# Two blocks per job transposed on VectorE in 32x32 parts and laid in place by transfers within SBUF

## The chip, the cores and the metric

One core of a Trainium2 chip runs the whole program as one launch. The metric is the time of one execution on the device in microseconds (us); the number before is the median of three runs. The engines are named as in the profile: PE is TensorE, PEld its loading of the stationary operand (it overlaps PE), DVE is VectorE, ACT is ScalarE, POOL is GpSimd, SP is SyncE, which here only issues transfers.

## The reference

Attention with a threshold, then two MLP layers, all in float32. Attention has 4 batches of 8 heads, 576 positions and 64 values per head; the MLPs have 2304 tokens, a model width of 512 and an inner width of 2048.

```
scores = q @ k.T / sqrt(64)
thresh = scores.max(-1) - tau
scores = where(scores >= thresh, scores, -1e9)
attn = exp(scores - scores.max(-1))
attn = attn / (attn.sum(-1) + 1e-9)
x = attn @ v                      # heads side by side: 2304 x 512
h = x @ w_in;  g = h if h >= 1, 0 if h <= -1, else (h + 1)**2 / 4;  x = g @ w_out
h = x @ w_in2; g = h * clip(h + 3, 0, 6) / 6;                        out = g @ w_out2
```

## The kernel before, in words

**Jobs, blocks, steps.** Attention is cut into 16 jobs, numbered from 0: a batch and a pair of heads each. A job has five blocks of query rows: four of 128 rows with both heads, and a last one with the 64 remaining rows of both heads. A step of the loop in `attention()` starts one block: step 5j+i starts block i of job j. Within a step, `em_scores` multiplies q by k on TensorE into two double banks P0 and P1 of PSUM (from job 10 on, JR, in three products of split operands), and VectorE moves the result to the tile p, with the row's extreme as a by-product (L395). `em_exp` lets ScalarE take the exponential (L408) and VectorE form the threshold (L411). `em_mask` multiplies by the threshold's mask on VectorE and sums the rows (L417). The tile p has three buffers and holds two heads of 2 x 288 columns; it has one query row on each partition.

**Turning a block.** The product with v needs the block transposed. A step later `em_pt` does this, once per head: four transposes of 128x128 on TensorE against the identity (issued by the helper `turn`, L294) into one bank of PSUM, and an evacuation by ScalarE (L445) into the tile Gf of the job's group. Group "a" holds blocks 0 and 1 (256 queries), group "b" blocks 2 to 4 (320). The last 64 key columns of both heads are turned by `em_tail` (L459, L463) into Gt. The banks Q0 and Q1 are taken by turns (`rotate`) by `em_pt`, `em_tail` and the product with v.

**The product with v.** When the last block of a group is turned, its five chunks go into the queue `pvq`: four chunks of 128 keys and the tail, each with one product per head (L481). `pv_chunk` runs them, and ScalarE moves the result to xu (L487). Gf and Gt have one buffer per group, so `turned` first runs what is left of the job before. `pv_run(5)` stands twice in a step, and a chunk runs at the earliest in the step behind the one that queued it. The normalisation (`pre_norm`, `fetch_norm`, `em_norm`) follows in steps 5j+5, 5j+6 and 5j+9; the row sums go through DRAM (L507, L522, L524).

**What runs beside attention.** Once the first batch is through, the first MLP layer (`dense1`) runs in between: at each `yield` of `attention()` it gets 0.57 credits (`share`), and pays 0.33 for each piece that it emits. A round works on 256 tokens; one value f of the inner width (an f-step) has twelve products into the one bank Q2 (`em_h`, L724), then ScalarE, VectorE (L735), ScalarE and POOL (L742) on the result, and twelve products of the output layer (`em_part`, L786) into Q3. There are 60 f-steps; what is left of them when attention ends runs behind it, followed by the rest of the first MLP and the second.

**What sets the order.** The Tile framework orders the instructions of each engine, in general by their place in the program, earlier where what stands before them is not ready. `pe_pins` lists attention's products in order; products of the MLP may not come before the last but one of them at the time of their emission, those with v not before the last. Scores after the first of a block are raised in priority. Each engine works through its queue in order.

**Queues.** All transfers here are issued by SP, in order. Loads of q and k for the job after the next are cut into strips of 32 columns (L233), since from job 4 on VectorE turns q and k in 32x32 parts (L304 for jobs from 10 on, 128x640). Loads of v are L281 and L282, stores of the first layer's partial sums L800.

**The tile w_c** in the pool `stage` has two buffers of 128x512 and serves the split of the MLP's weights (`split_a`, `split_b`). The weights that the first rounds need are split before job 10; the next ones follow behind attention.

Of the kernel before, what the change touches and what calls it, by code (L numbers as in the profile page):

```python
# [8 lines left out]
F32 = mybir.dt.float32  # L9
# [9 lines left out]
def kernel(  # L19
# [12 lines left out]
    nc = tc.nc  # L32
    V, S, G, T = nc.vector, nc.scalar, nc.gpsimd, nc.tensor
    NB, NH, SEQ, D = q.shape
# [4 lines left out]
    MAIN = 512  # L39
    TAIL = SEQ - MAIN  # L40
# [7 lines left out]
    NF1 = 10  # L48
    NAT = 1
    JT = 4  # L50
    JR = 10
    MLAG = 2
    RAW = 3
# [4 lines left out]
    stage = ctx.enter_context(tc.tile_pool(name="stage", bufs=1))  # L58
# [138 lines left out]
    NBLK = 5  # L197
    HEADS = range(2)
# [4 lines left out]
    AFTER = {1: "a", 4: "b"}  # L203
# [13 lines left out]
    vn = [ap.tile([128, 5, 2, D], F32, name=f"vn{i}") for i in range(2)]  # L217
# [22 lines left out]
    def load_q(j):  # L240
# [4 lines left out]
        for h in HEADS:  # L245
            src = q[b, 2 * hp + h]
            if j >= JR:
                strips(qn, 0, src[0:MAIN, :], h)
                strips(qn, 16 + 2 * h, src[MAIN:SEQ, :], h)
                continue  # L250
            if j >= JT:
                strips(qn, 0, src, h)
# [100 lines left out]
    zt, gt, xu, p_t = {}, {}, {}, {}  # L353
# [59 lines left out]
    def em_mask(j, i):  # L413
        p, nm, th, es = blk.pop((j, i))
        for x, e in enumerate(es):
            z = zcol(x, i)
            pins["M"] = V.scalar_tensor_tensor(out=p[:, x], in0=p[:, x], scalar=th[:, x:x + 1], in1=e,  # L417
                                            op0=ALU.is_le, op1=ALU.mult, accum_out=zt[j][:, z:z + 1])
        p_t[j, i] = p.rearrange("p h e n -> p (h e n)")

    def turned(j, g):
        if (g, j) not in gt:
            n = GROUPS[g][0]
            while (g, j - 1) in gt:
                pv_chunk()
            gt[g, j] = (ap.tile([128, 2, 4, n], F32, tag=f"G{g}", name="Gf"),
                        ap.tile([128, n], F32, tag=f"T{g}", name="Gt"))
        return gt[g, j]

    def rotate():  # L430
        mode["r"] = 1 - mode.get("r", 0)
        return bank(f"Q{mode['r']}")

    def em_pt(j, i, h):

        p = p_t[j, i]
        g, d0 = PARTS[i]
        f = turned(j, g)[0]
        mode["n"] += 1
        tm = rotate() if mode["mlp"] else bank("Q0" if mode["n"] % 2 else "Q2")  # L440
        p0 = h * (SEQ + TAIL)
        for cc in range(4):
            turn(tm[:, cc * 128:(cc + 1) * 128], p[:, p0 + cc * 128:p0 + (cc + 1) * 128], cc == 0)
        if i < NBLK - 1:
            S.activation(out=f[:, h, :, d0:d0 + 128], in_=tm.rearrange("p (c n) -> p c n", c=4), func=ACTF.Copy)  # L445
        else:
            for x in HEADS:
                S.activation(out=f[:, x, :, d0:d0 + TAIL],
                                      in_=tm.rearrange("p (c h n) -> p h c n", c=4, h=2)[:, x], func=ACTF.Copy)
# [16 lines left out]
    o_t, pvq = {}, []  # L466

    def pv_chunk():

        j, g, c = pvq.pop(0)  # L470
        n, d0 = GROUPS[g]
        f, t = gt[g, j]
        if c == 0:
            if j not in xu:
                here.pop(j - XLIVE, None)
                xu[j] = here[j] = mt.tile([128, SEQ], F32, tag="xu", name="xu", bufs=XLIVE)
            o_t[j, g] = rotate() if mode["mlp"] else bank("Q1")
        o = o_t[j, g][:, 0:n]
        for h in (1, 0):
            with tc.high_priority(offset=0 if h else 900):  # L480
                mm = T.matmul(o[h * D:(h + 1) * D], vn[j % 2][:, c, h, :], f[:, h, c] if c < 4 else t,  # L481
                              start=(c == 0), stop=(c == 4), skip_group_check=True)
            after(mm, pe_pins[-1] if h else prev)
            prev = mm
        if c == 4:
            del gt[g, j], o_t[j, g]
            S.activation(out=xu[j][:, d0:d0 + n], in_=o, func=ACTF.Copy)  # L487
# [28 lines left out]
    def fetch_norm(j):  # L516
        if j not in rbs or j not in OVER:
            return
        rd, rb = rbs[j]
        for h in HEADS:  # L520
            r = slice(64 * h, 64 * h + 64)
            nc.sync.dma_start(out=rb[r, 0:MAIN].rearrange("p (c n) -> p c n", c=4),  # L522
                              in_=rd[4 * h:4 * h + 4, :].unsqueeze(0).to_broadcast([64, 4, 128]))
            nc.sync.dma_start(out=rb[r, MAIN:SEQ], in_=rd[8:9, r].to_broadcast([64, 64]))  # L524
# [35 lines left out]
    def attention():  # L560

        order = [(j, i) for j in range(NJ) for i in range(NBLK)]
        n = len(order)
        turns, tailq, maskq = [], [], []
        plan = {}

        def at(t, what, *x):
            plan.setdefault((t, what), []).append(x)

        for j in range(NJ):  # L570
            at(NBLK * j + (4 if j < HP - 1 else 3), "q", j + 1)
            at(NBLK * j + 4, "k", j + 1)
            at(NBLK * j + NBLK + 0, "z", j)
            at(NBLK * j + NBLK + 1, "f", j)
            at(NBLK * j + NBLK + 4, "n", j)

        def now_at(what):
            return plan.get((t, what), [])

        def masked():  # L580
            while maskq:
                b = maskq.pop(0)
                em_mask(*b)
                turns.append(b)
                tailq.append(b)

        def due(lag):
            r = []
            while turns and (len(turns) > lag or t >= n):
                r.append(turns.pop(0))  # L590
            return r

        def tails(lag):
            while tailq and (len(tailq) > lag or t >= n):
                em_tail(*tailq.pop(0))

        for t in range(n + 6):
            mode["t"] += 1
            mode["step"] = True
            if not mode["mlp"]:  # L600
                if t < n:
                    em_scores(*order[t])
                    maskq.append(order[t])
                pv_run(2)
                yield
                if t < n:
                    em_exp(*order[t], 0)
                    em_exp(*order[t], 1)
                masked()
                for x in now_at("z"):  # L610
                    pre_norm(*x)
                for x in now_at("f"):
                    fetch_norm(*x)
                yield
                now = due(1)
                for b in now:
                    em_pt(*b, 0)
                    yield
                for x in now_at("q"):
                    unit_q(*x)  # L620
                    yield
                for b in now:
                    if b[1] < NBLK - 1:
                        em_pt(*b, 1)
                        yield
                for b in now:
                    if b[1] in AFTER:
                        pvq.extend((b[0], AFTER[b[1]], c) for c in range(5))
                pv_run(3)
                for x in now_at("k"):  # L630
                    unit_k(*x)
                    yield
                tails(1)
                for x in now_at("n"):
                    em_norm(*x)
                    yield
            else:
                if t < n:
                    em_scores(*order[t])
                    maskq.append(order[t])  # L640
                    em_exp(*order[t], 0)
                    em_exp(*order[t], 1)
                for x in now_at("z"):
                    pre_norm(*x)
                for x in now_at("f"):
                    fetch_norm(*x)
                masked()
                yield
                for x in now_at("n"):
                    em_norm(*x)  # L650
                    yield
                now = due(1)
                tails(1)
                pv_run(5)
                yield
                for x in now_at("q"):
                    unit_q(*x)
                    yield
                for b in now:
                    em_pt(*b, 0)  # L660
                    yield
                pv_run(5)
                for b in now:
                    if b[1] < NBLK - 1:
                        em_pt(*b, 1)
                        yield
                for x in now_at("k"):
                    unit_k(*x)
                    yield
                for b in now:  # L670
                    if b[1] in AFTER:
                        pvq.extend((b[0], AFTER[b[1]], c) for c in range(5))


# [172 lines left out]
    steps, o = [], 0  # L847
    while o < len(outs):
        n = len(steps)
# [139 lines left out]
    for _ in attention():  # L989
# [11 lines left out]
        while credit > 0:  # L1001
            c = next(part1)
# [388 lines left out]
```

## Time and profile before

| What | Value |
|---|---|
| Median of three runs | 1105.09 us (1104.98 to 1105.69) |
| Profiled execution, its own time | 1104.55 us |
| Span of the profiled execution | 1102.8 us |
| Mean granted clock of TensorE | 0.993 of full speed |
| PE busy | 1069.6 us (97%), 6514 products |
| PEld busy | 876.3 us (79%) |
| DVE busy | 670.0 us (61%), 1313 instructions |
| ACT busy | 641.3 us (58%), 1271 instructions |
| POOL busy | 452.1 us (41%), 390 instructions |
| Moved by transfers | 132.54 MB in 175019 packets |

The busy time of an engine is the union of its instructions' spans. Matmuls are pipelined, and a single one's span is longer than what it adds to the queue. The span lies inside the execution's own time; 1.75 us of that are ahead of the first instruction or behind the last. Shares over the whole span are means over stages with different limits, so the stretch in which the change lies has to be looked at by itself.

### The profile page before, as it was taken

Reading aid. Unit: us, or ns where it says so; the run is one execution under the profiler, and the core shown is the slowest. Engines: PE = TensorE matmul, PEld = TensorE weight load, DVE = VectorE, ACT = ScalarE, POOL = GpSimd, SP = SyncE. Lnnn points to the kernel's source line nnn. Section 1 sums busy time; section 2 is a strip of 40 time slices with the busy share of each in tenths; the row PEclk is TensorE's granted clock in tenths of the full one; section 3 lists DMA queues with packets and bytes.
Section 4 is the critical chain, followed back from the end, with each engine's and each line's share of the span. In section 5 each row is a group of like instructions: output and inputs, shape, how many; then the busy total and the mean of one; then the engine's idle time right before and its main releaser. Section 6 shows DMA issues by size and latency. Waiting matters only on the chain.

```text
span 1102.8 us, 18304 instructions
## 1 busy us (share of the span) xinstructions
PE 1069.6 (97%) x6514; PEld 876.3 (79%) x6514; DVE 670.0 (61%) x1313; ACT 641.3 (58%) x1271; POOL 452.1 (41%) x390
## 2 busy tenths in 40 slices
PE   7998889999999999999999999999999999999998
PEld 5555567778888888888889888888888888887887
DVE  5889998975776756355536855657788633333010
ACT  5777886776767767555557766555444433334221
POOL 0233767733222222155627665567623211112432
PEclk9999899999999999999999999999999999999999
DMA  6444545333322121125223555555455155449211
GB/s 170 121 96 104 130 103 149 70 73 82 72 61 66 45 62 42 32 67 161 88 88 124 174 182 190 170 174 170 125 182 190 53 187 161 157 149 374 66 39 58
DMA packets 175019, 132.54 MB, mean 120 GB/s; under 512 B 102736, under 2 KB 142416, under 8 KB 174928
## 3 DMA queue, kind: packets, MB, share of 16 engines
q1 hardware_dynamic: 173584, 131.08, 40.5%
q8 instruction: 51, 0.84, 0.3%
q10 hardware_dynamic: 1344, 0.30, 0.1%
q14 instruction: 40, 0.33, 0.1%
HBM read 93.00 MB, written 38.34 MB: 119 GB/s over the span
## 4 chain that ended last, share of the span: by engine, by line
PE 76%; issue 9%; DVE 8%; POOL 3%; ACT 3%; DMA 1%; SPq 0%; DVEq 0%; POOLq 0%; ACTq 0%
PE Q L724 25%; PE P L766 18%; PE Q L786 7%; PE Q L481 6%; PE P L380 5%; PE Q L294 5%; PE P L1164 4%; DVE p L395 2%; DVE p L417 2%; PE Q L1290 2%; PE Q L1301 2%; POOL gl L1153 2%; PE Q L1184 1%; DVE xl L705 1%; ACT e L408 1%
## 5 line engine op out<-in xcount | busy, mean ns | idle before, releaser
L742 POOL TENSOR_TENSOR gl<-r,gh 128x256 fp32r<-128x256 f32 (+1 forms) x142 | 154.4, 1088 | 290.9 <-ACT gh L741 279.4
L724 PE MATMUL Q<-xh,wih 128*128 128x256 f32 (+1 forms) x568 | 193.5, 341 | 2.5 <-DVE r L735 2.3
L724 PE MATMUL Q<-xl,wih 128*128 128x256 f32 (+1 forms) x568 | 188.9, 332 | 0.0
L724 PE MATMUL Q<-xh,wil 128*128 128x256 f32 (+1 forms) x568 | 188.8, 332 | 0.0
L417 DVE SCALAR_TENSOR_TENSOR p<-p,th,e 128x576 f32<-128x576 f32 x144 | 123.2, 877 | 15.5 <-ACT e L408 9.7
L408 ACT ACTIVATE e<-p,nm 128x576 f32<-128x576 f32 x144 | 109.4, 775 | 35.3 <-DVE p L395 34.4
L735 DVE SCALAR_TENSOR_TENSOR r<-r,Q 128x256 f32<-128x256 f32 (+1 forms) x110 | 54.8, 498 | 121.6 <-ACT r L734 117.6
L724 PEld LDWEIGHTS Q<-xh,wih 128*128 128x128 f32 x568 | 107.6, 189 | 20.3 <-DVE r L735 4.1
L741 ACT ACTIVATE gh<-r 128x256 fp32r<-128x256 f32 (+1 forms) x142 | 73.0, 515 | 82.4 <-DVE r L735 31.1
L294 PE MATMUL Q<-ident,p 128*128 128x128 f32 x656 | 106.9, 280 | 10.4 <-ACT Gf L445 8.1
L724 PEld LDWEIGHTS Q<-xl,wih 128*128 128x128 f32 x568 | 107.7, 190 | 10.3
L724 PEld LDWEIGHTS Q<-xh,wil 128*128 128x128 f32 x568 | 107.5, 189 | 10.2
L143 POOL TENSOR_TENSOR w_c<-w_c,w_raw 128x512 int32<-128x512 int32 x64 | 89.6, 1400 | 42.6 <-DVE w_c L141 21.8
L294 PEld LDWEIGHTS Q<-ident,p 128*128 128x128 f32 x656 | 73.7, 140 | 40.0 <-ACT Gf L445 14.3
L1153 POOL TENSOR_TENSOR gl<-r,gh 128x512 fp32r<-128x512 f32 x32 | 41.6, 1302 | 137.9 <-ACT gh L1152 137.9
L380 PE MATMUL P<-kt,qt 64*128 64x288 f32 (+2 forms) x508 | 83.8, 416 | 11.7 <-DVE p L395 9.6
L445 ACT ACTIVATE Gf<-Q 128x512 f32<-128x512 f32 x128 | 74.1, 594 | 15.9 <-PE Q L294 15.1
L1184 PE MATMUL Q<-xw,sw 128*128 128x512 f32 x336 | 80.7, 389 | 0.2 <-DVE C L1200 0.2
L733 ACT ACTIVATE r<-Q,half 128x256 f32<-128x256 f32 (+1 forms) x110 | 58.7, 535 | 32.4 <-PE Q L724 25.0
L786 PE MATMUL Q<-gh,woh 128*128 128x256 f32 x240 | 75.3, 314 | 1.4 <-DVE ob L799 1.4
L395 DVE TENSOR_SCALAR_CACHE_REDUCE p<-P 128x576 f32<-128x576 f32 x90 | 65.2, 750 | 17.2 <-PE Q L294 10.1
L1184 PEld LDWEIGHTS Q<-xw,sw 128*128 128x128 f32 x336 | 63.0, 188 | 13.5 <-DVE C L1200 0.4
(147 smaller groups left out, 2455.2 us busy)
## 6 DMA issues: line engine op xcount, KB each, us to landing
sw<-sd SPq DMA_DIRECT2D x88, 256.0 KB
w_raw<-in_moe_w_in_dram SPq DMA_DIRECT2D x32, 512.0 KB
w_raw<-in_moe_w_out_dram SPq DMA_DIRECT2D x32, 512.0 KB
sd<-wz SPq DMA_DIRECT2D x32, 256.0 KB
vn<-in_v_dram SPq DMA_DIRECT2D x32, 128.0 KB
x2p<-ob SPq DMA_DIRECT2D x16, 256.0 KB
x2d<-ob SPq DMA_DIRECT2D x16, 256.0 KB
sd<-wih SPq DMA_DIRECT2D x16, 256.0 KB
```

Of the source, the lines that this page charges most:

```text
L143: x = G.tensor_tensor(out=c.bitcast(I32), in0=c.bitcast(I32), in1=r, op=ALU.add)
L294: x = T.transpose(out, in_, ident)
L380: mm = T.matmul(o, a[j][r, cs], w[j][r, k0:k0 + HS], start=(n == 0), stop=(n == len(terms) - 1), skip_group_check=True)
L395: reads(V.tensor_scalar(out=p[:, x], in0=s[:, :, 0:HS], scalar1=taus[:, 3:4] if j >= JR else -1.0, scalar2=3e38, op0=ALU.mult, op1=ALU.min ...
L408: pins["S"] = S.activation(out=e, in_=p[:, x], func=ACTF.Exp, bias=nm[:, x:x + 1], scale=-1.0)
L417: pins["M"] = V.scalar_tensor_tensor(out=p[:, x], in0=p[:, x], scalar=th[:, x:x + 1], in1=e, op0=ALU.is_le, op1=ALU.mult, accum_out=zt[j][ ...
L445: S.activation(out=f[:, h, :, d0:d0 + 128], in_=tm.rearrange("p (c n) -> p c n", c=4), func=ACTF.Copy)
L724: mm = T.matmul(h, l[:, kk * 128:(kk + 1) * 128], r, start=(x == 0), stop=(x == 3 * KD - 1))
L742: y = G.tensor_tensor(out=gl, in0=r, in1=f32(gh), op=ALU.subtract)
L766: T.matmul(a, l, r, start=(first and x == 0), stop=(last and x == 2))
L786: mm = T.matmul(o, l, r, start=(f == fs[0] and x == 0 and i == 0), stop=(f == fs[-1] and x == 2 and i == 1), skip_group_check=True)
L1184: T.matmul(banks[role], t[:, l, c, :], r, start=(first and y == 0), stop=(y == 5), skip_group_check=True)
```

## The change

For jobs 10 to 15 (`JD = 10`), blocks 0 and 1 no longer go through `em_pt`. In the step behind the block's own, between its scores' and exponentials' emission and the masks of the step's own block, `place` turns each head's 512 main columns on VectorE: one instruction on 128x512 that transposes 32x32 parts, reading key columns with a step of four words, into a tile y (tag w_c, two buffers). Four transfers per head, all issued by SP, then lay 32 partitions of y (32 x 512) as 128 partitions of 128 into Gf, which this group now holds in another order: 8 parts of 32 queries, each with the four chunks. `chunk` gives the product with v its view of that: eight runs of 32 words. The `yield`s of the dropped `em_pt` calls fall away with them. The chunks of group "a" are queued when block 2 is turned, and no longer when block 1 is. The tails stay on TensorE. Jobs 0 to 9, and blocks 2 to 4, stay as they are.

```diff
+    JD = 10
...
+    def place(j, i):
+
+        p = p_t[j, i]
+        f = turned(j, "a")[0].rearrange("p h c n -> p h (c n)")
+        for h in HEADS:
+            p0 = h * (SEQ + TAIL)
+            y = stage.tile([128, MAIN], F32, tag="w_c", name="pb", bufs=2)
+            V.transpose(out=y.rearrange("p (g c k) -> p g c k", g=4, c=4),
+                        in_=p[:, p0:p0 + MAIN].rearrange("p (c k g) -> p g c k", c=4, g=4))
+            for a in range(4):
+                c = (4 * i + a) * 128
+                E = nc.sync
+                E.dma_start(out=f[:, h, c:c + 128], in_=y[32 * a:32 * a + 32, :].rearrange("k (g x) -> k g x", g=4))
+
+    def chunk(f, j, g, h, c):
+        if j >= JD and g == "a":
+            return f[:, h].rearrange("p c n -> p (c n)").rearrange("p (s c n) -> p c s n", c=4, n=32)[:, c]
+        return f[:, h, c]
...
-                mm = T.matmul(o[h * D:(h + 1) * D], vn[j % 2][:, c, h, :], f[:, h, c] if c < 4 else t,
+                mm = T.matmul(o[h * D:(h + 1) * D], vn[j % 2][:, c, h, :], chunk(f, j, g, h, c) if c < 4 else t,
...
+        placeq = []
+
+        def placed():
+            while placeq:
+                place(*placeq.pop(0))
+
         def masked():
             while maskq:
                 b = maskq.pop(0)
                 em_mask(*b)
+                if b[0] >= JD and b[1] < 2:
+                    placeq.append(b)
...
+                placed()
                 masked()
...
                 for b in now:
-                    em_pt(*b, 0)
-                    yield
+                    if not (b[0] >= JD and b[1] < 2):
+                        em_pt(*b, 0)
+                        yield
                 pv_run(5)
                 for b in now:
-                    if b[1] < NBLK - 1:
+                    if b[1] < NBLK - 1 and not (b[0] >= JD and b[1] < 2):
                         em_pt(*b, 1)
                         yield
...
                 for b in now:
-                    if b[1] in AFTER:
+                    if b[0] >= JD and b[1] in (1, 2):
+                        if b[1] == 2:
+                            pvq.extend((b[0], "a", c) for c in range(5))
+                    elif b[1] in AFTER:
                         pvq.extend((b[0], AFTER[b[1]], c) for c in range(5))
```

## Rows read from the trace of the kernel before

**Rows 1.** Busy time by stretch: stretch, length, five engines, PEclk, DMA share, GB/s

```profile
273.00:447.00 174.00, 172.44 (x1477) 148.44 (x1479) 119.97 (x315) 122.67 (x270) 44.61 (x44) 1.00 0.24 59
447.00:480.00 33.00, 32.98 (x239) 28.95 (x236) 7.53 (x17) 17.10 (x41) 5.79 (x9) 1.00 0.03 11
302.00:331.40 29.40, 27.84 (x234) 23.73 (x234) 22.05 (x55) 18.84 (x42) 8.07 (x8) 1.00 0.27 62
60.00:80.00 20.00, 17.73 (x124) 10.82 (x126) 17.33 (x49) 14.81 (x32) 6.21 (x6) 1.00 0.51 96
100.00:120.00 20.00, 15.94 (x96) 9.77 (x94) 19.57 (x46) 15.42 (x35) 9.82 (x9) 0.83 0.36 89
```

**Rows 2.** Chain of waits, 360 to 392 us: start, us, engine, tile, line, count

```profile
by line: PE Q L786 23.5%; PE Q L481 20.8%; PE Q L724 20.8%; PE P L380 17.9%; PE Q L294 17.2%
...
361.46 0.99 PE P L380 x12
...
363.87 0.44 PE Q L294 x4
...
366.08 0.36 PE Q L786 x3
...
366.88 0.99 PE P L380 x12
...
369.29 1.43 PE Q L724 x12
...
379.47 0.99 PE P L380 x12
...
387.21 2.31 PE Q L481 x20
```

**Rows 3.** Groups of instructions, 273 to 447 us: busy us, mean ns, idle before

```profile
L294 PE MATMUL Q<-ident,p 128*128 128x128 f32 x246 | 40.5, 277 | 0.0
...
L445 ACT ACTIVATE Gf<-Q 128x512 f32<-128x512 f32 x48 | 28.4, 595 | 10.4 <-PE Q L294 9.9
```

**Rows 4.** Lines L304 and L504, whole run: duration ns min/median/max

```profile
L304 DVE STREAM_TRANSPOSE raw<-kn x6: 832/840/841, 238.6 to 387.8; 128x640 f32<-128x640 f32 x6
...
L504 DVE STREAM_TRANSPOSE rq<-rp x14: 166/211/213, 27.5 to 420.0; 128x32 f32<-128x32 f32 x14
```

**Rows 5.** Lines L141 and L738, whole run

```profile
L141 DVE SCALAR_TENSOR_TENSOR w_c<-w_raw,w_c x64: 677/693/1908, 26.5 to 787.8; 128x512 uint32<-128x512 uint32 x64
...
L738 DVE SCALAR_TENSOR_TENSOR r<-r,Q x32: 670/680/691, 709.4 to 881.2; 128x512 f32<-128x512 f32 x32
```

**Rows 6.** Timeline of VectorE over one block: start us, us, what

```profile
345.15 0.42 DVE L735 SCALAR_TENSOR_TENSOR r<-r,Q 128x256 f32<-128x256 f32 x1
345.50 0.82 DVE L395 TENSOR_SCALAR_CACHE_REDUCE p<-P,taus 128x576 f32<-128x576 f32 x1
...
346.24 0.81 DVE L395 TENSOR_SCALAR_CACHE_REDUCE p<-P,taus 128x576 f32<-128x576 f32 x1
...
347.43 0.82 DVE L417 SCALAR_TENSOR_TENSOR p<-p,th,e 128x576 f32<-128x576 f32 x1
...
348.18 0.82 DVE L417 SCALAR_TENSOR_TENSOR p<-p,th,e 128x576 f32<-128x576 f32 x1
348.92 0.08 DVE L417 DVE_READ_ACCUMULATOR p<-p,th,e 128x1 f32 x1
```

**Rows 7.** Timeline of SP's queue in job 12

```profile
332.50 1.66 SPq L507 DMA_DIRECT2D rd<-rq  x4
335.49 0.46 SPq L524 DMA_DIRECT2D rb<-rd  x1
...
339.10 3.86 SPq L233 DMA_DIRECT2D kn<-in_k_dram  x5
343.06 3.92 SPq L233 DMA_DIRECT2D qn<-in_q_dram  x8
```

**Rows 8.** Line L481, 273 to 447 us: instructions on TensorE's sequencer

```profile
L481 PEldq EVENT_SEMAPHORE  x12: 51/51/51, 284.8 to 442.2; - x12
```

## The prediction

> **What bounds the kernel now.** I read the busy time by stretch first. Jobs eleven to sixteen run from 273 to 447 us, 174 us for six jobs, 29.0 us each. [...] One piece of it, 302 to 331.4, loses 1.56 us of TensorE; the stage behind attention (447 to 480) loses nothing [rows 1]. Then the chain of waits: in a window of the stretch it holds TensorE's lines alone, in five shares, of which the transposes L294 are 17.2% [rows 2]. So TensorE sets the end there: a microsecond taken off its queue is a microsecond off the end, as long as it never waits for anything else. VectorE has 174 - 119.97 = 54.0 us free, 9.0 per job. [...]
>
> **Removed.** For two blocks of six jobs, two heads each, `em_pt` falls away: 24 groups of four transposes on TensorE and 24 evacuations L445 on ScalarE. A group stands in the chain with 0.44 us [rows 2]. The mean of one transpose, 277 ns [rows 3], is its pipelined length and not what it takes from the queue. 24 x 0.44 = 10.56 us off TensorE, all of it on the path. ScalarE loses 24 x 0.595 = 14.3 us [rows 3]; nobody waits for it there, so I put that at nothing.
>
> **Moved work.** Each dropped `em_pt` also drops a yield, and a yield buys the first MLP layer 0.57 credits. 24 x 0.57 = 13.7 credits. One f-step takes eight pieces of 0.33, or 2.64, so 5.2 f-steps move behind attention. One costs twelve products of L724, 1.43 us, and twelve of L786, four pieces of three with 0.36 [rows 2], together 2.9; 15 us of TensorE leave the stretch of six jobs and are paid behind it, where TensorE is full already. Net nothing, if the stretch gets shorter by as much. This is the point on which the sum turns: the stretch holds 15 + 10.6 us less of TensorE's work, and attention must run that much faster, 24.7 us a job (174 - 25.6, over six).
>
> **Added on VectorE.** 24 transposes of 128x512, read with a step of four words. The same operation on contiguous words takes 840 ns for 640 columns and 211 ns for 32 [rows 4], 1.03 ns a column, so 0.71 us for 512. Below: 0.71 (no row gives a reason for less). Above: no row reads with such a step. A step of two words costs nothing: L141, which reads every second word, has a median of 693 ns, L738 on contiguous words 680 [rows 5]. I take as upper end one word every second slot, 512 x 2 x 1.03 plus the fixed 0.18, or 1.24 us. I take 0.71, because the operation is the same and the nearest stepped row is free; 2.8 us per job, 17 in all.
>
> [...]
>
> **What VectorE's load does to the pace.** One block needs, from L395 at 345.50 to the last accumulator read at 349.00, 3.5 us of VectorE, plus L735 with 0.42: 3.92 [rows 6]. Place puts two transposes between the scores and the masks of the second and the third step of a job: 3.92 + 1.42 = 5.34 a step, 10.7 for both. On TensorE the second step's scores stand at 366.88 and the fourth step's at 379.47, 12.59 us apart [rows 2]. Each of these two steps loses two groups (0.88) and two yields (two times 0.57/0.33 pieces of 0.36 us [rows 2], 1.24), so 12.59 - 2 x 2.12 = 8.35. TensorE is then 2.3 us a job short of work there, against a VectorE that is slower. On the other side the product with v of the first group, 2.31 us [rows 2], moves a step later, to the stretch behind the first step's scores. This was 361.46 to 366.88, 5.42 us, and becomes 7.7 against 3.92 on VectorE: 3.8 us of work that can slide into the short steps, as far as the order of the queue lets it (MLP products are pinned to the last but one of attention's, the product with v to the last). Between no cover and full cover the price is 13.8 and 0 us over six jobs. I take half, 1.15 a job, 6.9 in all: over a whole job VectorE needs 120/6 - 0.4 (less MLP) + 2.8 = 22.4 of 24.7 us, so there is room on the mean, but one stretch lost 1.56 us with VectorE at 22.05 of 29.4 [rows 1].
>
> **Added on the queues.** 96 transfers of 64 KB within SBUF, eight per block, on SP. An issue takes 0.41 us (rd, 1.66 for four) to 0.77 (k, 3.86 for five) [rows 7]: 3.3 to 6.2 us per block, two blocks a job. SP is nearly full from 335.5 to 347 in the job shown, with loads of k and q [rows 7]. These are needed a job later, so place's transfers delay nothing that is due; they themselves have until the product, two steps on. What they hold is the tile y (two buffers): the next block's first transpose waits until four transfers of the block before have landed, 5 us later, and behind it on VectorE stand that step's masks and the next L395. Four issues are 3.1 us at most and a landing was seen within 1.3 us (L507's last issue ends at 334.16, L524 that reads it starts at 335.49) [rows 7], so 4.4 of the 5.3 us of a step; I put it at nothing, and as a rival where SP is full. The rest: products read runs of 32 words instead of contiguous 256; nothing in the rows prices that, between 0 and a doubling of 48 x 0.115 us (20 in 2.31 [rows 2]), 5.5 us; I take 0, since a run is far longer than the step that L141 reads for nothing. Waits for more semaphores cost 51 ns each on TensorE's queue [rows 8], a few per job, hidden behind running products.
>
> **Sum.** -10.56 + 6.9 = -3.7 us. Against the profiled execution's 1104.55 that is 1100.9; the median of the runs shown, 1105.09, stands 0.5 above it, so 1101.4. A measurement of this kernel can tell about 0.2%, 2.2 us, from no change.
>
> **Rivals.** *VectorE has room.* TensorE slides enough work into the short steps (3.8 us are there for 2.3), and no pace is lost: -10.5 to -9, 1095. For it: 9 us a job free now. Against it: the 1.56 us lost at 302 to 331. Chance 0.18.
>
> *The stepped read doubles the transposes, and VectorE becomes the bound: slower.* At 1.24 us a step needs 6.4 us, both 12.8 against TensorE's 8.35: 4.5 a job short, and over a job VectorE needs 24.6 of 24.7 us. With half of it covered, 13.4 us are given back: +2.8, 1108; with none covered, 26.7: +16, 1121. Between these it decides at 10.56/6 = 1.76 us given back per job; with half covered that is reached at 0.95 us for one transpose. For it: nothing in the trace reads with such a step, and VectorE does set the pace once it is full [rows 1]. Against it: L141. Chance 0.26. [...]
>
> *Transfers land late, no change.* In the three jobs in which k and q are still loaded, SP is busy when place issues; should the second block's transposes stand 3 us behind y each time, 9 us come back: -1, 1104. For it: SP's busy stretch falls on the second and third step. Against it: loads that are not due can go behind. Chance 0.14.
>
> That the transposes would not leave TensorE is excluded by the code.
>
> **How the numbers follow.** My forecast (0.42) holds 1097 to 1104: 0.31 of it is faster by over 0.2%, 0.11 within. With the first rival's 0.18 faster is 0.49. Within: 0.11 + 0.12 of the third rival = 0.23. Slower: 0.26 + 0.02 of the third = 0.28. The range goes from the first rival's 1095 to 1109, just over the second's half-covered price; beyond stay its dearer end (0.12) and the cheap tail (0.05).
>
> **What would show it.** L294 with 96 transposes less and L445 with 24 less; the new transposes' mean at 0.7 us (right) or 1.2 (second rival). VectorE near 22 us of a job of 26 us. TensorE's idle time in the short steps, behind L395, 5 to 9 us over the six jobs: none would be the first rival, over 11 the second. VectorE waiting for a DMA before a transpose would be the third. About 15 us of L724 and L786 more behind attention's last mask. The forecast is wrong if the six jobs take under 150 or over 158 us (155 by the sum: 174 - 15 - 3.7), or if TensorE waits for the laid parts themselves.

## The result and the profile after

The changed kernel takes 1112.58 us in the median of five runs (1109.37 to 1116.24), the kernel before 1105.09 (1104.25 to 1105.69). The ratio is 1.0064 with a 95% interval of 1.0050 to 1.0078, so the change costs 7.1 us (the two medians lie 7.5 apart; the ratio is what all figures below go by). The forecast was 1101.4 with a range from 1095 to 1109, and the sign is the other one.

The profiled execution is the quickest of the five, 1109.37 us, with a span of 1107.5 against 1102.8. The trace thus shows 4.7 of the 7.1 us. Why the runs of the changed kernel spread over 7 us, where those before spread over 1.4, stays open.

Stretches of the changed kernel, with columns as in [rows 1]:

```profile
273.00:441.30 168.30, 157.81 (x1294) 130.44 (x1292) 139.43 (x328) 105.51 (x233) 42.46 (x40) 0.98 0.41 95
270.00:480.00 210.00, 199.47 (x1628) 168.69 (x1627) 159.32 (x368) 130.31 (x294) 57.93 (x57) 0.98 0.36 85
364.00:368.00 4.00, 2.49 (x14) 2.31 (x15) 4.00 (x8) 1.25 (x4) 0.73 (x1) 0.77 0.41 68
368.00:372.00 4.00, 4.00 (x27) 2.57 (x26) 3.86 (x11) 3.41 (x8) 0.00 (x0) 0.80 0.48 104
404.00:408.00 4.00, 2.10 (x15) 2.13 (x16) 3.86 (x11) 1.72 (x4) 1.13 (x2) 0.89 0.49 107
408.00:412.00 4.00, 4.00 (x26) 4.00 (x25) 1.65 (x5) 2.06 (x5) 0.00 (x0) 0.68 0.18 40
366.50:369.50 3.00, 2.97 (x14) 2.75 (x16) 2.86 (x7) 2.50 (x6) 0.73 (x1) 0.50 0.31 67
407.50:410.50 3.00, 3.00 (x16) 3.00 (x16) 1.95 (x7) 1.29 (x3) 0.00 (x0) 0.50 0.28 63
```

The stretch 270 to 480 of the kernel before, which the experiments below are set against:

```profile
270.00:480.00 210.00, 208.42 (x1742) 179.27 (x1741) 128.38 (x335) 141.29 (x316) 52.10 (x53) 1.00 0.21 51
```

TensorE sits idle for 210 - 199.47 = 10.5 us, where it was 1.6. It also loses clock. The four windows of 4 us have a mean below 1.00, because the granted clock is 0.50 for a part of them, as the last two rows show. By the means it loses about 2.49 x 0.23 + 4.00 x 0.20 + 2.10 x 0.11 + 4.00 x 0.32 = 2.9 us. So 8.9 + 2.9 = 11.8 us of TensorE are lost, more than the 10.56 that were taken off it. Attention's last instruction on its row sums (the tile z, L500 before and L520 now), at 446.2 us before, comes at 441.4, 4.8 earlier; the prediction's sum had some 18.7 (15 moved and 3.7 gained). The six jobs take 168.3 us, where I had called the forecast wrong beyond 158.

Who waits for whom, 273 to 445 us of the changed kernel: engine, tile and line, then the releaser with us in total, times and the longest. First VectorE:

```profile
DVE pb L438 <- DMA Gf<-pb: 7.0, 4, 2.6
DVE p L418 <- ACT e L409: 4.6, 9, 0.7
DVE p L396 <- PE P L381: 3.8, 3, 2.3
DVE raw L305 <- DMA rd<-rq: 2.9, 2, 1.7
DVE raw L305 <- DMA qn<-in_q_dram: 2.7, 1, 2.7
...
DVE raw L305 <- DMA kn<-in_k_dram: 1.8, 1, 1.8
```

Then TensorE:

```profile
PE Q L295 <- DVE p L418: 5.3, 4, 2.7
PE P L381 <- DVE p L396: 3.1, 3, 1.4
PE Q L757 <- DVE r L768: 2.0, 3, 1.4
```

VectorE, with 139.43 of 168.30 us busy, stands still for 7.0 us before the new transposes (L438), until the transfers have emptied y, and for 2.9 + 2.7 + 1.8 = 7.4 us before L305, the transposes of q and k, where the releaser named is a DMA. Not all of the 7.4 is new: in the kernel before, VectorE stood 1.9 us for a DMA at the same line (L304 there). Behind the waiting instruction in the same queue stand the masks (L418) and the moving of the scores (L396), and those two make up 8.4 of TensorE's 10.4 us of waits. SP's queue in jobs 12 and 13:

```profile
335.54 5.10 SPq L443 DMA_DIRECT2D Gf<-pb  x8
340.68 0.59 SPq L234 DMA_DIRECT2D kn<-in_k_dram  x1
341.60 5.74 SPq L443 DMA_DIRECT2D Gf<-pb  x8
...
354.49 3.49 SPq L234 DMA_DIRECT2D qn<-in_q_dram  x7
358.07 1.37 SPq L527 DMA_DIRECT2D rd<-rq  x4
...
360.21 0.66 SPq L234 DMA_DIRECT2D qn<-in_q_dram  x1
...
366.56 10.79 SPq L443 DMA_DIRECT2D Gf<-pb  x16
```

The 16 issues of a job stand almost in a row, 10.8 us of the queue. Behind those of job 12 the loads of q that stood at 343 to 347 us in [rows 7] stand at 354 to 361. In the kernel before, the transpose that reads them, the last one below, starts at 362.7 (L304 of that kernel, 273 to 445 us):

```profile
L304 DVE STREAM_TRANSPOSE raw<-qn x4: 845/846/846, 272.9 to 362.7; 128x640 f32<-128x640 f32 x4
```

So these loads were needed some 16 us after the last of them was issued, and they now come 11 to 14 us later. The groups of the tile pb, 200 to 480 us, show the price of one issue and one transpose (min, median and max of their duration in ns):

```profile
L443 SPq DMA_DIRECT2D Gf<-pb x96: 543/602/1272, 284.6 to 432.8; - x96
L438 DVE STREAM_TRANSPOSE pb<-p x24: 1055/1108/1136, 282.1 to 429.8; 128x512 f32<-128x512 f32 x24
```

The chain of waits through one of the gaps, 364 to 376 us (start, us, what):

```profile
365.16 1.02 DVE pb L438
...
366.56 0.59 SPq L443
...
367.20 0.59 SPq L443
...
367.85 0.60 SPq L443
...
368.49 2.18 DMA Gf<-pb
...
371.14 0.57 DVE pb L438
...
373.48 1.12 DVE pb L438
```

In [rows 2] the chain was TensorE's alone. Here it goes from a transpose through three of its issues (366.56 to 368.49) and 2.18 us from the start of the fourth to its landing, at 370.67, to the next transpose, and TensorE is not in it. An issue takes 0.60, so the landing comes 1.6 us behind the end of the fourth issue.

How a stall begins is seen in VectorE's timeline; the bracket gives the idle time ahead of the instruction and what ended it. The first is the wait for q, the second the longest wait for y:

```profile
362.54 0.85 DVE L305 STREAM_TRANSPOSE raw<-qn 128x640 f32<-128x640 f32 x1 [2.75 <-DMA qn<-in_q_dram]
...
363.60 0.82 DVE L418 SCALAR_TENSOR_TENSOR p<-p,th,e 128x576 f32<-128x576 f32 x1
...
398.44 1.10 DVE L438 STREAM_TRANSPOSE pb<-p 128x512 f32<-128x512 f32 x1 [2.59 <-DMA Gf<-pb]
```

And what TensorE does with it, in its own timeline:

```profile
361.36 0.28 PE L819 MATMUL Q<-gh,woh 128*128 128x256 f32 x1
361.48 0.28 PE L819 MATMUL Q<-gl,woh 128*128 128x256 f32 x1
...
365.31 0.30 PE L295 MATMUL Q<-ident,p 128*128 128x128 f32 x1 [1.83 <-DVE p L418]
...
367.12 0.41 PE L757 MATMUL Q<-xh,wil 128*128 128x256 f32 x1
367.33 0.41 PE L757 MATMUL Q<-xh,wih 128*128 128x256 f32 x1
...
405.90 0.30 PE L295 MATMUL Q<-ident,p 128*128 128x128 f32 x1 [2.75 <-DVE p L418]
```

The load of q is late, VectorE stands 2.75 us before L305, the masks start that much later, and TensorE waits 1.83 us for them. Products that started 0.12 us apart start 0.21 us apart in the row 366.5 to 369.5 above, at the granted clock of 0.50.

### The profile page after: what moved, and what is told of

It reads as the page before. It is cut to its first block, busy times and chain, and to the rows that moved or that the text cites. A ratio compares the mean times of both kernels' runs of the same rounds, so it can differ in the third digit from the quotient of the medians.

```text
span 1107.5 us, 18290 instructions
## 1 busy us (share of the span) xinstructions
PE 1066.5 (96%) x6418; PEld 871.8 (79%) x6418; DVE 685.6 (62%) x1337; ACT 629.8 (57%) x1247; POOL 451.8 (41%) x390
## 4 chain that ended last, share of the span: by engine, by line
PE 72%; DVE 12%; DMA 5%; SPq 3%; ACT 3%; issue 3%; POOL 1%; DVEq 0%; POOLq 0%; ACTq 0%
PE Q L757 22%; PE P L799 18%; PE P L1197 7%; PE Q L1217 6%; PE Q L819 5%; DVE p L396 4%; PE Q L501 4%; PE P L381 3%; DVE p L418 3%; PE Q L295 2%; PE Q L1323 2%; PE Q L1334 2%; DMA sw<-sd 2%; DVE pb L438 1%; ACT e L409 1%
## 5 line engine op out<-in xcount | busy, mean ns | idle before, releaser
L418 DVE SCALAR_TENSOR_TENSOR p<-p,th,e 128x576 f32<-128x576 f32 x144 | 125.4, 892 | 15.1 <-ACT e L409 9.5
L295 PE MATMUL Q<-ident,p 128*128 128x128 f32 x560 | 93.4, 283 | 15.6 <-DVE p L418 7.7
L295 PEld LDWEIGHTS Q<-ident,p 128*128 128x128 f32 x560 | 63.3, 141 | 45.7 <-issue 18.0
L381 PE MATMUL P<-kt,qt 64*128 64x288 f32 (+2 forms) x508 | 83.2, 413 | 13.9 <-DVE p L396 11.8
L396 DVE TENSOR_SCALAR_CACHE_REDUCE p<-P 128x576 f32<-128x576 f32 x90 | 65.2, 751 | 20.0 <-PE Q L295 11.9
L1217 PEld LDWEIGHTS Q<-xw,sw 128*128 128x128 f32 x336 | 63.0, 188 | 13.4 <-DVE C L1233 0.4
L501 PE MATMUL Q<-Gf,vn 128*64 128x320 f32 (+1 forms) x512 | 72.5, 423 | 0.0
```

The source lines that it names most:

```text
L295: x = T.transpose(out, in_, ident)
L381: mm = T.matmul(o, a[j][r, cs], w[j][r, k0:k0 + HS], start=(n == 0), stop=(n == len(terms) - 1), skip_group_check=True)
L396: reads(V.tensor_scalar(out=p[:, x], in0=s[:, :, 0:HS], scalar1=taus[:, 3:4] if j >= JR else -1.0, scalar2=3e38, op0=ALU.mult, op1=ALU.min ...
L501: mm = T.matmul(o[h * D:(h + 1) * D], vn[j % 2][:, c, h, :], chunk(f, j, g, h, c) if c < 4 else t, start=(c == 0), stop=(c == 4), skip_gro ...
L1217: T.matmul(banks[role], t[:, l, c, :], r, start=(first and y == 0), stop=(y == 5), skip_group_check=True)
```

## The experiments

Two explanations stand against each other from the start. By the first, the transfers do the harm: VectorE stands at an instruction that waits for a DMA (for y to be emptied, or for q and k), with masks and scores behind it. By the second, it is the pace: the dropped yields and the later product with v leave TensorE too little to do, whatever the transfers do. The price of the stepped read is a question beside both. Ratios are to the kernel before, measured on the same chip, with 95% intervals in brackets; us are worked out as (ratio - 1) x 1105.09.

**Without the transfers.**

```diff
-            for a in range(4):
-                c = (4 * i + a) * 128
-                E = nc.sync
-                E.dma_start(out=f[:, h, c:c + 128], in_=y[32 * a:32 * a + 32, :].rearrange("k (g x) -> k g x", g=4))
+            if i == 0 and h == 0:
+                nc.sync.dma_start(out=f.rearrange("p h n -> p (h n)"), in_=q[0].rearrange("h s d -> (h s d)")[0:128 * 2048].rearrange("(p n) -> p n", n=2048))
```

> Leaves out the 16 transfers of a job that lay the turned parts in place; one load of 1 MB of q into the group's tile stands for them, so the products with v read other data. The transposes, their tile y and the dropped yields stay. Theory Q (SP's queue: 16 issues of 0.60 us a job, and what waits behind them or for their landing, hold VectorE and so TensorE): falls from 1112.6 to 1098 to 1104 us, at or below the kernel before (1105.1), and VectorE's 14 us of waits for a DMA in jobs ten to fifteen shrink below 4. Theory V (VectorE's added 26.6 us of transposes set the pace): stays at 1109 to 1113. Theory P (the dropped yields leave TensorE without work in the short steps): stays at 1109 to 1113.

Measured 1100.15 us, 0.9943 [0.9922, 0.9964]: -6.3 us. The change without its transfers is faster than the kernel before. From this run to the change it is 13.4 us: that is the transfers' price. The load that stands for them moves the same 1 MB a job into the same tile (88 GB/s in 270 to 480 us, 85 with the transfers), so it is not the number of bytes that costs this.

**Half of the issues on ScalarE's queue.**

```diff
-                E = nc.sync
+                E = nc.scalar if h else nc.sync
```

> The second head's transfers are issued by ACT's queue instead of SP's; all else as in the change. Theory Q: SP has 8 issues less a job, 4.8 us, and both heads' parts are issued side by side: 1105 to 1109 us. Theories V and P: 1111 to 1114, or more if ACT's exponentials are held up by its issues.

Measured 1111.16 us, 1.0053 [1.0036, 1.0069]; its interval overlaps the change's. An issue has a median of 582 ns there and 602 on SP, so the same number of issues now stands on two queues, one of them with ScalarE's own work behind it. VectorE's waits for a DMA shrink from 14.4 to 2.5 us (273 to 445 us), and yet nothing is gained: TensorE now waits 3.8 us for evacuations by ScalarE (xu and Gt), for which it does not wait in the change, and 4.6 us for VectorE. The run's time tells nothing apart; that the issues on ScalarE's queue hold up its evacuations instead is what the waits suggest, and no run tests it.

**The read without its step** (the wrong key columns are taken, 512 in a row).

```diff
-                        in_=p[:, p0:p0 + MAIN].rearrange("p (c k g) -> p g c k", c=4, g=4))
+                        in_=p[:, p0:p0 + MAIN].rearrange("p (g c k) -> p g c k", g=4, c=4))
```

> The transposes read their 512 columns contiguously instead of with a step of four words, so the parts land in another order and the product with v is of other data; counts, sizes and waits stay. If the step is what makes 128x512 take 1.11 us, one transpose takes 0.70 to 0.75 us here; otherwise it stays at 1.1. Theory V: 24 x 0.4 = 9.6 us of VectorE less, 1103 to 1107 us. Theories Q and P: 1110 to 1113.

Measured 1109.33 us, 1.0033 [1.0023, 1.0042]: 3.4 us less than the change. The tile pb in this run:

```profile
L438 DVE STREAM_TRANSPOSE pb<-p x24: 665/708/714, 283.4 to 431.2; 128x512 f32<-128x512 f32 x24
...
  DMA Gf<-pb: 13.0, 8
```

The step makes 0.708 us into 1.108. With short transposes VectorE only comes sooner to a tile that is not empty yet and waits 13.0 us for it, where it was 7.0. The run lies between the ranges expected. Without its step the change is still 3.7 us slower than the kernel before, so the stepped read is at most a part of the loss.

**The yields kept**, outside the conditions around `em_pt`.

```diff
-                        yield
+                    yield
```

and the same for the second `em_pt`.

> The two yields that the dropped turning calls had are kept, so the first MLP layer gets its 13.7 credits back in these steps and about 15 us of TensorE's work moves back beside attention. Theory P: TensorE has work while VectorE and the transfers catch up: 1097 to 1104 us, at or below the kernel before. Theory Q: the steps are longer, so part of the waiting is hidden: 1105 to 1110. Theory V: 1108 to 1112.

Measured 1112.11 us, 1.0055 [1.0035, 1.0075]; the interval lies over the change's. TensorE idles no less, 13.5 us:

```profile
270.00:480.00 210.00, 196.47 (x1608) 165.26 (x1605) 149.66 (x354) 126.63 (x283) 49.44 (x50) 0.99 0.34 78
```

The dropped yields are not the cause.

**A third buffer** for one of the four tiles of a job.

```diff
-            y = stage.tile([128, MAIN], F32, tag="w_c", name="pb", bufs=2)
+            y = (mt.tile([128, MAIN], F32, tag="before", name="pb", bufs=1) if i and not h else stage.tile([128, MAIN], F32, tag="w_c", name="pb", bufs=2))
```

> A third tile y: the second block's first head writes into a tile that the first MLP layer no longer needs by then, so its transpose does not wait for the first block's transfers to land. Theory Q1 (what hurts is VectorE standing at the tile y until transfers have landed, with masks and scores behind it): the 7.0 us of waits at the transposes fall below 2 and the time to 1104 to 1108 us. Theory Q2 (what hurts is SP itself: 16 issues of 0.60 us in a row push the loads of k and q and the sums' trip through DRAM back, whatever the buffers): 1110 to 1113.

Measured 1107.67 us, 1.0022 [1.0007, 1.0037]: 4.6 us less than the change. The wait for y falls from 7.0 to 2.1 us; those for q and k stay (2.8 and 2.3).

**The loads of q and k on ScalarE's queue**, for jobs 11 to 15.

```diff
-            nc.sync.dma_start(out=flat[p0:p0 + 32, 32 * s0:32 * (s0 + n)].rearrange("p (s d) -> p s d", d=32),
+            (nc.scalar if mode.get('act') else nc.sync).dma_start(out=flat[p0:p0 + 32, 32 * s0:32 * (s0 + n)].rearrange("p (s d) -> p s d", d=32),
...
+        mode['act'] = j > JD
```

> The loads of q and k for jobs eleven to fifteen (16 issues a job) go to ACT's queue; the 16 transfers of the laid parts stay on SP with two tiles y. Theory Q2: SP is free for the laid parts, no load comes late: 1103 to 1107 us. Theory Q1: the tile y still has to wait for its own eight issues and the landing: 1109 to 1112. If ACT's 7 us of issues a job cost more than they free: above 1112.

Measured 1103.49 us, 0.9989 [0.9975, 1.0004]: 8.3 us less than the change, level with the kernel before. VectorE waits for no load of q or k any more, and still 6.4 us for y.

**All of the transfers on GpSimd's queue** (`E = nc.gpsimd`).

> All 96 transfers of the laid parts are issued by POOL's queue, which is busy a quarter of this stretch; SP has the work that it had before. Theory Q2: 1100 to 1105 us, if POOL's issues take no longer than SP's. Theory Q1: still 1108 to 1112, as y waits for landing all the same. POOL's multiply of xu and its subtractions stand behind the issues: if that decides, above 1112.

Measured 1106.76 us, 1.0014 [1.0004, 1.0023]: 5.5 us less than the change, with an issue at 552 ns and 1.8 us of waits for y. It lies between the two ranges expected. Freeing SP helps from this side too.

**A control: the kernel before with the same loads on ScalarE's queue** (the edit of the run with the loads, for `j > 10`).

> The control for the run with the loads of q and k on ACT: the kernel before, with nothing of the change, but these loads on ACT's queue. If their move is worth something by itself: 1099 to 1103 us. If it only makes room on SP for the laid parts (theory Q): 1104 to 1107, the kernel before with SP less busy and TensorE still full.

Measured 1108.41 us, 1.0032 [1.0020, 1.0044]. Moving the loads is no gift in itself: here it costs 3.5 us, beside place's transfers it brings 8.3. So the loads and place's transfers harm each other on one queue, and that is worth 11.8 us between the two pairs of runs. Both expectations missed: neither had the control slower. Where the 3.5 us come from, with TensorE as busy as before in 270 to 480 (208.33 us), stays open. In its profiled execution, 5.7 us longer in span, 2.6 us are there before the first moved load is issued at 215.1 us (the row sums of job 7 at 215.0 against 212.4), so in that execution not all of the loss can be the loads' doing.

**Loads moved and third buffer together.**

> The change with both reliefs: loads of q and k for jobs eleven to fifteen on ACT, and the third tile y. If the waits at y (theory Q1, worth 4.6 us alone) and the full queue (Q2, worth 8.0 alone) are two costs: 1097 to 1101 us, the 1100 of the run without transfers or near it. If they are the same cost seen twice: 1103 to 1105.

Measured 1103.85 us, 0.9990 [0.9981, 0.9998]. Of the DMA waits of VectorE 0.8 us are left, and yet it is no better than with the loads moved alone: the 4.6 and the 8.3 us are not two prices that add up, but as it seems the same idle time of TensorE, reached from two sides. TensorE still loses something:

```profile
270.00:480.00 210.00, 203.40 (x1678) 174.17 (x1677) 166.36 (x376) 135.37 (x303) 63.75 (x62) 0.99 0.37 87
```

**The same, with the yields kept as well.**

> As the run with both reliefs, and the yields of the dropped calls kept. Theory P's second chance: once the queue is no longer the bound, MLP work in the short steps fills what VectorE leaves open: 2 to 5 us below the run with both reliefs. If a short step is bound by VectorE and not by a lack of work on TensorE: within 2 us of it.

Measured 1106.61 us, 1.0012 [1.0003, 1.0021], apart from 0.9990 on the side that neither expectation had. Keeping the yields costs 2.4 us once both reliefs are in.

**The same, with the product with v queued a block earlier**, as before the change.

```diff
-                    if b[0] >= JD and b[1] in (1, 2):
-                        if b[1] == 2:
-                            pvq.extend((b[0], "a", c) for c in range(5))
-                    elif b[1] in AFTER:
+                    if b[1] in AFTER:
```

> As the run with both reliefs, but the product with v of the first group is queued as in the kernel before, a block earlier. If the laid parts have landed by then, the time stays within 2 us of the run with both reliefs; if they haven't, TensorE stands at the product (its queue is in order) and it is 3 to 8 us above.

Measured 1107.77 us, 1.0022 [1.0012, 1.0032]: 3.5 us more. The laid parts are not always there a block earlier: TensorE waits for their landing twice, 0.9 us together. Where the rest of the 3.5 comes from was not shown. Both parts of the pace are thus better as the change has them, and the second explanation falls.

**Two of the four transfers per head left out.**

```diff
-            for a in range(4):
+            if i == 0 and h == 0:
+                nc.sync.dma_start(out=f.rearrange("p h (i a n) -> p h i a n", i=2, a=4)[:, :, :, 2:4, :].rearrange("p h i a n -> p (h i) (a n)"), in_=q[0].rearrange("h s d -> (h s d)")[0:128 * 1024].rearrange("(p s n) -> p s n", s=4, n=256))
+            for a in range(2):
```

> Two of the four transfers of each head are left out (8 issues a job instead of 16, and one load of 0.5 MB for the rest of the group's tile), so half of the products' data is other. If the cost of the transfers is even in their number: half way between 1100 and 1112.6, 1105 to 1108 us. If it appears only when the queue is full: 1100 to 1103.

Measured 1105.49 us, 1.0005 [0.9996, 1.0014]. From none to half it is 6.9 us, from half to all 6.5: the price goes about with their number. The first eight a job cost as much as the last eight, so half of them are not hidden either.

**No transfers, and the read without its step.**

> No transfers, as in the first experiment, and the contiguous read of the third: transposes of 0.71 us. The products' data is other. If the slower transposes are what keeps the run without transfers (1100.2) from the full saving on TensorE: 1095 to 1098 us, near the first rival's 1095. If VectorE had room there and the rest is something else: 1099 to 1101.

Measured 1096.70 us, 0.9927 [0.9912, 0.9942]: -8.1 us. The stretch 270 to 480 of this run:

```profile
270.00:480.00 210.00, 208.35 (x1708) 177.82 (x1707) 159.19 (x381) 140.11 (x310) 69.27 (x65) 1.00 0.34 91
```

The same stretch of the run without transfers that kept the step:

```profile
270.00:480.00 210.00, 204.88 (x1682) 174.67 (x1681) 167.50 (x377) 135.97 (x304) 66.13 (x63) 0.99 0.32 88
```

With transposes of 0.702 us TensorE is as busy as in the kernel before (208.42) at a granted clock of 1.00: no pace is lost to VectorE. With 1.106 us it idles 5.1 us, and the time is 1.8 us longer, though the two intervals overlap and the profiled execution with the step is the slowest of its four (1103.05 us), so that the 1.8 is not clear of the noise. In the run with neither, attention's last instruction on z comes at 427.4 us, 18.8 earlier than before, and the part of the span behind it is 10.7 longer: 8.1 net, as timed.

**Third buffer, and the loads on GpSimd's queue.**

> The change with the third tile y and the loads of q and k for jobs eleven to fifteen issued by POOL's queue, which has the most room, instead of ACT's. If the ACT issues cost what the control showed (3.5 us): 1099 to 1102, faster than the kernel before. If POOL's subtractions for q and k then come late: 1104 or more.

Measured 1122.96 us, 1.0174 [1.0148, 1.0201]. VectorE now waits for GpSimd's own work on q and k, 6.1 and 5.5 us, in a queue that holds the issues too (waits of VectorE, 273 to 445 us, in the slowest of the five executions; L307 is L305 of the change):

```profile
DVE raw L307 <- POOL ql L309: 6.1, 2, 4.0
...
DVE raw L307 <- POOL kl L309: 5.5, 4, 2.2
```

GpSimd, on whose results VectorE depends, is a worse place for these issues than a full SP (1.0174 here, 1.0022 with the third buffer alone).

**Both heads in one tile**: y has 128x1024 (the two buffers of w_c as one tile wcp), and four transfers of 128 KB per block do what eight of 64 KB did.

```diff
...
-            for a in range(4):
-                c = (4 * i + a) * 128
-                E = nc.sync
-                E.dma_start(out=f[:, h, c:c + 128], in_=y[32 * a:32 * a + 32, :].rearrange("k (g x) -> k g x", g=4))
+        for a in range(4):
+            c = (4 * i + a) * 256
+            nc.sync.dma_start(out=f[:, c:c + 256],
+                              in_=wcp[32 * a:32 * a + 32].rearrange("k x n -> k (x n)").rearrange("k (g x) -> k g x", g=4))
...
```

> The whole computation of the change with both heads in one transfer: the transposes interleave the two heads' parts in one tile of 128x1024 (the two halves of which the weight splits use in turn), and four transfers of 128 KB a block lay them, 8 issues a job instead of 16, the same bytes. If the number of issues is the price: 1104 to 1107 us, like the run with half of the transfers left out. If the bytes and the landing are: 1110 to 1113.

Measured 1107.74 us, 1.0022 [1.0013, 1.0031]: 4.6 us less than the change at the same bytes, between the two ranges expected. The issues, in the groups of the tile wcp, 200 to 480 us:

```profile
L444 SPq DMA_DIRECT2D Gf<-wcp x48: 542/602/1281, 285.9 to 429.9; - x48
```

The wait for the tile, 273 to 445 us, columns as for the waits above:

```profile
DVE wcp L440 <- DMA Gf<-wcp: 6.7, 5, 2.5
```

An issue takes the same 602 ns with twice the bytes, so half the issues are half of SP's time. But one tile is one buffer, and the waits for it are back at 6.7 us.

**The same, with the loads on ScalarE's queue.**

> As the run with both heads at once, with the loads of q and k for jobs eleven to fifteen on ACT's queue. If what is left of the price is SP's queue: 1099 to 1103 us, faster than the kernel before; if the ACT issues cost as much as they free, no faster than the run with both heads at once.

Measured 1106.71 us, 1.0011 [1.0002, 1.0021], with 7.2 us of waits for the tile: no better, to within the intervals. None of the versions that keep the whole computation is clearly faster than the kernel before; the best, 0.9990 [0.9981, 0.9998] and 0.9989 [0.9975, 1.0004], lie within 0.2% of it. A layout in which the transpose reads contiguous words and the output stays the reference's wasn't tried.

## Why the prediction was wrong, step by step

The ledger from the runs: the removal with everything kept short -8.1 us, the stepped read +1.8, the transfers +13.4; together the measured +7.1. These are the steps from the kernel before through two runs to the change, so they add up by construction, and the middle one is not clear of the noise.

**What bounds the kernel: right**, and its condition decided. "A microsecond taken off its queue is a microsecond off the end, as long as it never waits for anything else": TensorE now waits 8.9 us more.

**Removed: right in kind, some 2.5 us too large in what it brought.** Over the whole run the transposes are 656 - 560 = 96 fewer and the evacuations 128 - 104 = 24 fewer, as said. The run without transfers and step brings 8.1 of the 10.56 us. Whether the rest is a mis-sized 0.44 us or the six loads of 1 MB in that run stays open.

**Moved work: right in mechanism, too large.** Behind attention's last row sum the products of 128x256 of each kind go from 46 to 54 in the first layer and from 48 to 65 in the output layer. With three kinds and 0.12 us each, (8 + 17) x 3 x 0.12 = 9.0 us, where I had 15; the span behind that point grows from 656.6 to 666.1 us, by 9.5. Why less was moved than the credits had it stays open.

**The transposes: 1.108 us**, between my 0.71 and the upper end of 1.24. I chose the lower end because L141, with a step of two words, stood at 693 ns against the 680 of L738 [rows 5]; a step of four words is not free. Without the step the run shows 0.708 us, the price that [rows 4] gave. So the step costs 0.40 us for 512 words, a factor of 1.56. The two slots for each word in my upper end were an estimate, which no run shows. The step's price to the end was 1.8 us without transfers and 3.4 with them, not the 13.4 to 26.7 of my second rival, which had the right sign for a wrong reason. (That rival's turning point is mis-reckoned too: 2 x 3.92 + 4 x 1.01 - 8.35 is twice 1.76, so it lies at 1.01 us for one transpose and not at 0.95; 1.108 is beyond both.)

**The pace: the 6.9 us given back were not.** Without the transfers, nothing is lost at 0.70 us per transpose, as the first rival had it; at 1.1 it is 1.8 us. I took half of the bound, although I had found 3.8 us of work to slide into a gap of 2.3.

**Added on the queues: the step that failed.** I wrote "These are needed a job later, so place's transfers delay nothing that is due", and of the wait for y "I put it at nothing". Together the transfers measured 13.4 us. Three things were wrong there.

- An issue takes 0.60 us, within my 0.41 to 0.77, but I counted it as 3.3 to 6.2 us per block, and not as 10.8 us in a row per job on a queue that was nearly full for part of each job.
- For the wait for y I counted one head's four issues and a landing of 1.3 us, 4.4 of the 5.3 us of a step. That much was right: from the first issue at 366.56 to the landing at 370.67 it is 4.1 us. But the second head's four issues stand behind the first's. Eight take 5.1 us, and with the same landing of 1.6 the second tile comes free 6.7 us after the first issue (an estimate from these rows), more than the step. Other issues can stand in between, too. The longest wait, 2.59 us in job 14, is one for the first head's tile, whose four issues were split by transfers of the row sums (SP's queue):

```profile
391.32 0.59 SPq L443 DMA_DIRECT2D Gf<-pb  x1
392.03 0.54 SPq L544 DMA_DIRECT2D rb<-rd  x1
392.67 1.17 SPq L542 DMA_DIRECT2D rb<-rd  x2
393.89 0.59 SPq L544 DMA_DIRECT2D rb<-rd  x1
394.52 10.74 SPq L443 DMA_DIRECT2D Gf<-pb  x15
```

- The loads behind the transfers do become due. They are needed some 16 us after the last issue and not a job of 29 later, and q came 2.75 us late for L305.

The third rival named the wait for y and SP's full stretch, and its sign, VectorE waiting for a DMA before a transpose, is what the trace shows. But it saw only one of the two waits and priced it at 9 us. Its sum of -1 also leaves out the 6.9 us of pace that stand in the forecast; with them it would have been +5.3, slower. The product's runs of 32 words, by contrast, cost nothing, as I took it: twenty of them still stand in the chain with 2.31 us.

**The clock** has no term in the sum: the idle time that I expected was small, and a stretch with gaps early in the run, 60 to 80 us, kept 1.00 [rows 1]. It cost about 2.9 us in the profiled execution, around gaps of 1.83 and 2.75 us.

How some 8 of the 13.4 us get to the end is shown by the trace of the change and by the two runs that free SP or y; which of the two waits does it in one execution is not separated, since curing both gains no more than curing one. After both, the transfers still cost 0.9990 - 0.9943, or 5.2 us. If the control's 3.5 us for loads on ScalarE's queue carry over, 1.7 remain; that sum is an argument and not a run.

## What to carry to other kernels

Moving work from the bounding engine to an idle one through transfers costs issue time on a queue (here 0.60 us for one, 10.8 us a job): add up all issues of a period on that queue, with what else is due from it in the same period, before anything is put at nothing. Ask of every wait on a DMA what stands behind it in the same engine's queue; here VectorE's mean load of 83%, with stalls of up to 2.75 us in the wrong place, left TensorE, which sets the end, idle for 10.5 us of 210. A control on the unchanged kernel keeps a helpful edit from being taken for the cause: here the same edit gained 8.3 us beside the transfers and lost 3.5 without them.

## What was unexpected of the hardware

- An issue on SP for a transfer within SBUF has a median of 602 ns for 64 KB and 602 ns for 128 KB; on ScalarE's queue it was 582 and on GpSimd's 552.
- A read with a step of four words makes a 128x512 transpose on VectorE 1.108 us instead of 0.708, though in another operation lines with and without a step of two words stand at 693 and 680 ns [rows 5].
- TensorE's granted clock fell to 0.50 from 366.5 to 369.5 us behind a gap of 1.83 us and from 407.5 to 410.5 behind one of 2.75, while from 60 to 80 us 2.3 us of idle time in all left it at 1.00 [rows 1].
